# Infini-attention with two feed-forward layers: the second layer's down products follow three items behind, and finished banks are copied out in the middle of an activation

## The chip, the cores and the metric

The kernel runs on one core of one Trainium2 chip. The metric is the device time of one execution in microseconds (us), as a median over runs. The core has five engines with a queue each: TensorE (PE in the rows, its weight loads are PEld), VectorE (DVE), ScalarE (ACT), GpSimd (POOL) and SyncE (SP), which issues most DMA transfers. An engine works through its queue in order and meets the others through semaphores.

## What is computed

The reference, cut to what matters:

```python
def reference(**kwargs):
    attn_out = _attn_ref(**attn_kwargs)            # causal attention mixed with a memory term, (4, 8, 576, 64)
    x = attn_out.transpose(0, 2, 1, 3).reshape(2304, 512)
    x = _moe_ref(x=x, **moe_kwargs)                # layer 1
    return _moe2_ref(x=x, **moe2_kwargs)           # layer 2

def _moe2_ref(x, w_in, w_out):                     # x 2304 x 512, w_in 512 x 2048, w_out 2048 x 512
    h = x @ w_in
    g = h - np.tanh(h)
    return (g @ w_out).astype(np.float32)
```

The change touches layer 2 alone.

## The kernel before, in words

Attention, the conversion of the weights and layer 1 are placed by a planner (`Schedule`), which writes their order from costs and due times; that part of the program is left as it is. Layer 2 follows it in an order written out by hand, in the loop of lines 1165 to 1175.

Layer 2 takes the tokens in rounds: four rounds of 512 tokens and a last one of 256 (`rounds`, line 1013). Inside a round the 2048 hidden columns are taken 128 at a time (`f`, 16 of them; in the last round two at a time). One such step is an item: 64 items of the wide rounds and 8 of the last one, 72 in all (`items`, lines 1151 and 1152). All matrix products are made in three parts (high by high, high by low, low by high), since each operand is held as a rounded part and a remainder.

For one item:

- `up2(i)` (L1116): 12 products on TensorE (24 narrower ones in the last round) write h, 128 hidden columns by 512 tokens, into one of four PSUM banks (`up2_p`, tile `up`).
- `act2(i)` (L1077 to L1097): ScalarE and VectorE turn h into g = h - tanh(h), by a polynomial for small values. ScalarE makes `u` (L1085), `w` (L1086), `w` again (L1090), `th` (L1091) and `mk` (L1092); VectorE makes `hu` (L1087), `gf` (L1093, L1094), takes `th` from h in place (L1095, tile `up`) and merges both (L1096), which ends the item's activation.
- `act2_end(i)` (L1099): the item's g is split: ScalarE writes the rounded part `gh` (L1103), and GpSimd the remainder `gl` (L412; VectorE for the last item). It is not issued with its own item but behind `u`, `w` and `hu` of the next one, through `state["late"]`.
- `down2(i)` (L1131, products at L1142): 12 products add g's share to the output banks `dn0` to `dn3`, three for each of four token tiles of 128 (two tiles in the last round, with six each). The four banks are a ring of one (`dn2_p`): a new round can write a bank only when the old one's contents have been copied out.
- `out_copy(r, k)` (L1123): when a round's last item has been added, bank k is copied to a tile `ob` (even k on ScalarE, L399; odd k on VectorE, L401), and SP sends it to memory (L1129). There are two `ob` tiles, so the third copy waits for the first tile's transfer and the fourth for the second's.
- `prep2` (L1154): at items 4, 6, 8 and 10 of a round the next round's input is loaded and split.

TensorE's order around an item is `up2(i)`, then `down2(i - LAG2)` with `LAG2 = 2`; the activation of item i and the round-end copies come from the loop:

```python
        if i < len(items):
            up2(i)
            act2(i)
...
        elif "late" in state:
            act2_end(*state.pop("late"))
        if i >= LAG2:
            down2(i - LAG2)
```

Of the kernel before, what the change touches and what calls it, by code (L numbers as in the profile page):

```python
# [244 lines left out]
def kernel(  # L245
# [165 lines left out]
    def low(e, out, in_, high):  # L411
        (nc.vector if e == "dve" else nc.gpsimd).tensor_tensor(out=out, in0=in_, in1=high, op=ALU.subtract)  # L412
# [418 lines left out]
        return first  # L831


    LAG2 = 2
    state = {}

    def up_mms(xs, ps, p):
# [185 lines left out]
    def load2(r, i):  # L1023
        x = late["x2"].tile([128, KT, 256], F32, name="x2i")
        nc.sync.dma_start(out=x, in_=x2s[rounds[r][i]])
        state[2, r, i, "x"] = x

    def split_hi(r, i, e):
        if i == 0:
            state[2, r, "xs"] = late["xs2"].tile([128, 2, KT, 512], F32R, name="xs")  # L1030
        xs, x = state[2, r, "xs"], state[2, r, i, "x"]
        copy(e, xs[:, 0, :, 256 * i:256 * i + 256], x)

    def split_lo(r, i):
        xs, x = state[2, r, "xs"], state.pop((2, r, i, "x"))
        part = slice(256 * i, 256 * i + 256)
        nc.vector.tensor_tensor(
            out=xs[:, 1, :, part], in0=x, in1=xs.bitcast(F32)[:, 0, :, part], op=ALU.subtract)
# [38 lines left out]
    def act2(i):  # L1077
        h = state.pop((2, i, "up"))
        u = t_p.tile([128, 512], F32, name="u")
        w = t_p.tile([128, 512], F32, name="w")  # L1080
        th = t_p.tile([128, 512], F32, name="th")
        hu = t_p.tile([128, 512], F32, name="hu")
        mk = t_p.tile([128, 512], F32, name="mk")
        g = t_p.tile([128, 512], F32, name="gf")
        nc.scalar.activation(out=u, in_=h, func=AF.Square)  # L1085
        nc.scalar.activation(out=w, in_=u, func=AF.Square, bias=sqb_t)  # L1086
        nc.vector.scalar_tensor_tensor(out=hu, in0=h, scalar=c4, in1=u, op0=ALU.mult, op1=ALU.mult)  # L1087
        if "late" in state:
            act2_end(*state.pop("late"))
        nc.scalar.activation(out=w, in_=w, func=AF.Square, bias=sqc_t)  # L1090
        nc.scalar.activation(out=th, in_=h, func=AF.Tanh)  # L1091
        nc.scalar.activation(out=mk, in_=u, func=AF.Relu, bias=thr_t)  # L1092
        nc.vector.scalar_tensor_tensor(out=g, in0=u, scalar=lin, in1=w, op0=ALU.mult, op1=ALU.add)  # L1093
        nc.vector.scalar_tensor_tensor(out=g, in0=g, scalar=off, in1=hu, op0=ALU.add, op1=ALU.mult)  # L1094
        nc.vector.tensor_tensor(out=h, in0=h, in1=th, op=ALU.subtract)  # L1095
        nc.vector.copy_predicated(out=g, mask=mk.bitcast(I32), data=h)  # L1096
        state["late"] = (i, g)  # L1097

    def act2_end(i, g):  # L1099
        gl = g2_p.tile([128, 512], F32R, name="gl")  # L1100
        gh = g2_p.tile([128, 512], F32R, name="gh")
        state[2, i, "g"] = (gh, gl)
        nc.scalar.activation(out=gh, in_=g, func=AF.Copy)  # L1103
        low("dve" if i == len(items) - 1 else "pool", gl, g, gh.bitcast(F32))

    def up2(i):
        r, fs = items[i]
        xs = state[2, r, "xs"]
        n = 512 // len(fs)
        ps = up2_p.tile([128, 512], F32, name="up")  # L1110
        state[2, i, "up"] = ps
        for s, f in enumerate(fs):
            w = wt[0][f]
            for kt in range(KT):
                for j, (wh, xh) in enumerate(((0, 0), (0, 1), (1, 0))):
                    nc.tensor.matmul(  # L1116
                        ps[:, s * n:(s + 1) * n], lhsT=w[:, wh * 512 + kt * 128:wh * 512 + (kt + 1) * 128],
                        rhs=xs[:, xh, kt, 0:n], start=(kt == 0 and j == 0), stop=(kt == KT - 1 and j == 2))

    def token_tiles(r):  # L1120
        return [(n, t) for n in rounds[r] for t in range(2)]

    def out_copy(r, k):  # L1123
        n, t = token_tiles(r)[k]
        last = r == len(rounds) - 1
        ob = ob_p.tile([128, 512], F32, name="ob")
        copy("dve" if k % 2 and not last else "act", ob, state["dn"][k])
        for j, (row, r0, nr) in enumerate(out_rows(n, t)):
            (nc.scalar if last and j else nc.sync).dma_start(out=out[row:row + nr, :], in_=ob[r0:r0 + nr, :])  # L1129

    def down2(i):  # L1131
        r, fs = items[i]
        if fs[0] == 0:
            state["dn"] = [dn2_p.tile([128, 512], F32, name=f"dn{k}") for k in range(len(token_tiles(r)))]
        gh, gl = state.pop((2, i, "g"))
        n = 512 // len(fs)
        end = fs[-1] == NF - 1
        for k, dn in enumerate(state["dn"]):
            for j, (g, wh) in enumerate(((gh, 0), (gh, 1), (gl, 0))):
                for s, f in enumerate(fs):  # L1140
                    c0 = s * n + k * 128
                    nc.tensor.matmul(  # L1142
                        dn, lhsT=g[:, c0:c0 + 128], rhs=wt[1][f][:, wh * 512:(wh + 1) * 512],
                        start=(fs[0] == 0 and s == 0 and j == 0), stop=(f == NF - 1 and j == 2))
            if end and r == len(rounds) - 1:
                out_copy(r, k)
        if end and r < len(rounds) - 1:
            for k in range(len(state["dn"])):
                out_copy(r, k)

    items = [(r, (f,)) for r in range(WIDE) for f in range(NF)]
    items += [(WIDE, (2 * p, 2 * p + 1)) for p in range(NP)]

    def prep2(r, step):  # L1154

        if r + 1 < len(rounds) and step // 2 < len(rounds[r + 1]):
            i = step // 2
            if step % 2 == 0:
                load2(r + 1, i)
            else:  # L1160
                split_hi(r + 1, i, "act")
                split_lo(r + 1, i)

    PREP = {4: 0, 6: 1, 8: 2, 10: 3}
    for i in range(len(items) + LAG2):
        if i < len(items):
            up2(i)
            act2(i)
            r, fs = items[i]
            if len(fs) == 1 and fs[0] in PREP:  # L1170
                prep2(r, PREP[fs[0]])
        elif "late" in state:
            act2_end(*state.pop("late"))
        if i >= LAG2:
            down2(i - LAG2)


# [42 lines left out]
```

## Time and profile before

| | |
|---|---|
| time, median of 3 runs | 1079.64 us (1079.57 to 1081.4) |
| the profiled execution's own time | 1081.9 us |
| its span | 1080.1 us |
| TensorE busy, matrix products | 1044.4 us, 97% of the span |
| VectorE, ScalarE, GpSimd busy | 757.9, 631.8 and 99.8 us |
| layer 2, first up product to the end | from 661.43 us on, about 419 us |

How to read it: a busy share is an average over the whole program. For a change to layer 2 alone, what counts is where TensorE stands still in layer 2 and for whom; the waits, the timeline and the table by stretches show that. Times in the rows are microseconds from the start of the span.

### The profile page before, as it was taken

To read this page: it belongs to the slowest core of one execution; us is meant where nothing else is said; L and a number is where in the kernel's file an instruction comes from. 1 tells how busy PE (TensorE), PEld (TensorE's weight loads), DVE (VectorE), ACT (ScalarE), POOL (GpSimd) and SP (SyncE) were. 2 spreads that over 40 slices of the span, in tenths; PEclk is the share of its full clock that TensorE was granted. 3 is DMA by queue.
4 is the path that set the end of the run, shared out by engine and by line. 5 is a ranking of instruction groups with operands and counts; after the bars stand their busy time and mean duration, and the time that the engine had idled before them with its cause. 6 is when DMAs were issued, how large, how long until landed. Compare 5 with 4: busy or idle time off the path is not lost.

```text
span 1080.1 us, 18824 instructions
## 1 busy us (share of the span) xinstructions
PE 1044.4 (97%) x6720; PEld 881.9 (82%) x6720; DVE 757.9 (70%) x2060; ACT 631.8 (58%) x1346; POOL 99.8 (9%) x102
## 2 busy tenths in 40 slices
PE   5799999999999999999999999999999999999997
PEld 3477798777779978979999998888788788878896
DVE  6999999878776587663221377776677677767775
ACT  6889876777673376362111124666566666666674
POOL 0001000000000000000000000222122122212221
PEclk9799999999999999999999999999999999999999
DMA  7867753555644354242100164000100100010010
GB/s 229 257 176 218 236 178 114 157 149 157 189 126 150 123 161 146 88 128 73 40 1 21 40 187 145 1 21 1 58 20 1 59 20 1 1 59 1 1 40 20
DMA packets 116397, 102.42 MB, mean 95 GB/s; under 512 B 63824, under 2 KB 92496, under 8 KB 116304
## 3 DMA queue, kind: packets, MB, share of 16 engines
q1 hardware_dynamic: 115088, 99.91, 30.5%
q10 hardware_dynamic: 1216, 1.31, 0.4%
q8 instruction: 53, 0.87, 0.3%
q14 instruction: 40, 0.33, 0.1%
HBM read 78.65 MB, written 22.54 MB: 94 GB/s over the span
## 4 chain that ended last, share of the span: by engine, by line
PE 64%; issue 20%; DMA 5%; ACT 5%; DVE 4%; SPq 1%; POOL 0%; DVEq 0%; ACTq 0%; POOLq 0%
PE up L1116 17%; PE dn L1142 17%; PE dn L947 9%; PE up L845 9%; PE s L703 3%; PE s L584 3%; PE o L725 3%; PE s L589 1%; PE o L670 1%; ACT e L630 1%; DMA qk<-in_qkt_dram 1%; DMA vs<-cv 1%; ACT e L647 1%; DMA w<-in_moe_w_in_dram 1%; PE s L547 1%
## 5 line engine op out<-in xcount | busy, mean ns | idle before, releaser
L845 PE MATMUL up<-xs,w 128*128 128x256 f32 x1728 | 236.4, 287 | 0.4 <-ACT g L924 0.4
L845 PEld LDWEIGHTS up<-xs,w 128*128 128x128 f32 x1728 | 217.6, 192 | 7.0 <-issue 5.6
L1116 PE MATMUL up<-xs,w 128*128 128x512 f32 (+1 forms) x960 | 214.4, 374 | 0.0
L1116 PEld LDWEIGHTS up<-xs,w 128*128 128x128 f32 x960 | 168.5, 188 | 35.2
L1142 PE MATMUL dn<-w,gh 128*128 128x512 f32 x576 | 179.2, 397 | 7.3 <-DVE ob L401 4.7
L947 PE MATMUL dn<-gh,w 128*128 128x256 f32 x1152 | 160.1, 286 | 0.0
L947 PEld LDWEIGHTS dn<-gh,w 128*128 128x128 f32 x1152 | 146.0, 192 | 7.2 <-issue 6.5
L1093 DVE SCALAR_TENSOR_TENSOR gf<-u,w 128x512 f32<-128x512 f32 x72 | 84.1, 1169 | 79.2 <-ACT w L1090 79.2
L412 POOL TENSOR_TENSOR gl<-gf,gh 128x512 fp32r<-128x512 f32 x71 | 91.7, 1292 | 512.3 <-ACT gh L1103 512.3
L924 ACT ACTIVATE g<-up 128x512 f32<-128x512 f32 x72 | 42.9, 595 | 160.8 <-PE up L845 145.6
L1142 PEld LDWEIGHTS dn<-w,gh 128*128 128x128 f32 x576 | 107.8, 189 | 34.8 <-DVE ob L401 7.3
L1085 ACT ACTIVATE u<-up 128x512 f32<-128x512 f32 x72 | 43.0, 598 | 120.8 <-PE up L1116 120.8
L1142 PE MATMUL dn<-w,gl 128*128 128x512 f32 x288 | 110.3, 392 | 0.6 <-POOL gl L412 0.6
L630 ACT ACTIVATE e<-e,mx 128x128 f32<-128x128 f32 (+4 forms) x144 | 82.7, 577 | 10.4 <-DVE mx L610 4.4
L401 DVE CAST gh<-g 128x512 fp32r<-128x512 f32 x36 | 15.4, 427 | 101.6 <-ACT g L924 101.6
L947 PE MATMUL dn<-gl,w 128*128 128x256 f32 x576 | 84.5, 285 | 0.0
L947 PEld LDWEIGHTS dn<-gl,w 128*128 128x128 f32 x576 | 75.2, 192 | 2.1 <-issue 1.9
L610 DVE CUSTOM_DVE_ANT_0 e<-s,mask 128x128 f32<-128x128 f32 (+4 forms) x144 | 63.7, 484 | 10.4 <-PE s L584 6.5
L703 PE MATMUL s<-identr,e 128*128 128x128 f32 x448 | 64.4, 289 | 4.3 <-ACT pT L399 2.8
L399 ACT ACTIVATE pt<-s 128x320 f32<-128x320 f32 (+4 forms) x149 | 58.2, 435 | 17.4 <-PE s L691 8.7
L584 PE MATMUL s<-qk 64*128 64x128 f32 (+3 forms) x256 | 55.8, 513 | 12.2 <-DMA qk<-in_qkt_dram 10.0
L1142 PEld LDWEIGHTS dn<-w,gl 128*128 128x128 f32 x288 | 54.4, 189 | 13.6 <-POOL gl L412 1.1
(101 smaller groups left out, 1435.9 us busy)
## 6 DMA issues: line engine op xcount, KB each, us to landing
w<-in_moe_w_out_dram SPq DMA_DIRECT2D x16, 512.0 KB, 5.1
cv<-in_moe_w_in_dram SPq DMA_DIRECT2D x32, 256.0 KB, 2.8
vs<-cv SPq DMA_DIRECT2D x64, 128.0 KB, 1.8
cv<-in_moe_w_out_dram SPq DMA_DIRECT2D x32, 256.0 KB, 2.8
w<-vs SPq DMA_DIRECT2D x32, 256.0 KB, 2.7
w<-in_moe_w_in_dram SPq DMA_DIRECT2D x14, 512.0 KB, 4.9
qk<-in_qkt_dram SPq DMA_DIRECT2D x16, 448.0 KB, 3.6
v<-in_v_dram SPq DMA_DIRECT2D x16, 320.0 KB, 3.6
```

The source lines that it names most:

```text
L399: nc.scalar.activation(out=out, in_=in_, func=AF.Copy)
L412: (nc.vector if e == "dve" else nc.gpsimd).tensor_tensor(out=out, in0=in_, in1=high, op=ALU.subtract)
L584: nc.tensor.matmul(ss[j].tile[:, c0:c0 + nn], lhsT=qk.tile[p, a:a + 128], rhs=qk.tile[p, kc:kc + nn], start=True, stop=True)
L610: nc.vector.tensor_tensor_reduce(out=out, in0=in0, in1=in1, scale=-scale, scalar=mx.tile[:, 0:1] if t == 4 and j else BIG, op0=ALU.add, op ...
L630: nc.scalar.activation(out=x, in_=x, func=AF.Exp, scale=-1.0, bias=mx.tile[:, k:k + 1], accum_out=sm.tile[:, j:j + 1])
L703: nc.tensor.transpose(ss[j].tile[:, a:a + 128], x, ident)
L845: nc.tensor.matmul(ps()[:, s, :], lhsT=w[:, wh * 512 + kt * 128:wh * 512 + (kt + 1) * 128], rhs=xs()[:, xh, kt, :], start=(kt == 0 and j = ...
L947: nc.tensor.matmul(dn[m // 2].tile[:, m % 2, :], lhsT=w[:, wh * 512 + m * 128:wh * 512 + (m + 1) * 128], rhs=gg.tile[:, s * 256:(s + 1) * ...
L1085: nc.scalar.activation(out=u, in_=h, func=AF.Square)
L1093: nc.vector.scalar_tensor_tensor(out=g, in0=u, scalar=lin, in1=w, op0=ALU.mult, op1=ALU.add)
L1116: nc.tensor.matmul(ps[:, s * n:(s + 1) * n], lhsT=w[:, wh * 512 + kt * 128:wh * 512 + (kt + 1) * 128], rhs=xs[:, xh, kt, 0:n], start=(kt = ...
L1142: nc.tensor.matmul(dn, lhsT=g[:, c0:c0 + 128], rhs=wt[1][f][:, wh * 512:(wh + 1) * 512], start=(fs[0] == 0 and s == 0 and j == 0), stop=(f ...
```

## The change

`LAG2` goes from 2 to 3. `act2` becomes a generator that stops once, behind `u`, `w`, `hu` and the late split of the item before; the loop runs it to that point, then issues `down2` of the item three behind (with the copies at a round's end), and then the rest of the activation. `prep2` moves behind `down2`. No instruction is added or taken away.

```diff
-    LAG2 = 2
+    LAG2 = 3
...
         if "late" in state:
             act2_end(*state.pop("late"))
+        yield
         nc.scalar.activation(out=w, in_=w, func=AF.Square, bias=sqc_t)
...
             up2(i)
-            act2(i)
-            r, fs = items[i]
-            if len(fs) == 1 and fs[0] in PREP:
-                prep2(r, PREP[fs[0]])
+            steps = act2(i)
+            next(steps)
         elif "late" in state:
             act2_end(*state.pop("late"))
         if i >= LAG2:
             down2(i - LAG2)
+        if i < len(items):
+            for _ in steps:
+                pass
+            r, fs = items[i]
+            if len(fs) == 1 and fs[0] in PREP:
+                prep2(r, PREP[fs[0]])
```

The line numbers behind line 1087 grow by one, and those of the loop by a few.

TensorE, at the start of layer 2 (`up` with `w_n` is the up product of item n, `dn` with `w_n` the down product of item n). Before:

```order
L1116 MATMUL up<-xs,w_0_276 128x512 x12
L1116 MATMUL up<-xs,w_1_329 128x512 x12
L1116 MATMUL up<-xs,w_2_534 128x512 x12
L1142 MATMUL dn_8899<-w_0_428,gh 128x512 x2
L1142 MATMUL dn_8899<-w_0_428,gl 128x512
```

Now:

```order
L1117 MATMUL up<-xs,w_0_276 128x512 x12
L1117 MATMUL up<-xs,w_1_329 128x512 x12
L1117 MATMUL up<-xs,w_2_534 128x512 x12
L1117 MATMUL up<-xs,w_3_592 128x512 x12
L1143 MATMUL dn_8925<-w_0_428,gh 128x512 x2
L1143 MATMUL dn_8925<-w_0_428,gl 128x512
```

Four items' up products now stand ahead of the first down product, where three stood. From there on each down product stands one item later.

ScalarE, at the end of the first round (`ob<-dn0` and `ob<-dn2` are the copies of banks 0 and 2). Before:

```order
L1085 ACTIVATE u_9567<-up_9554 128x512
L1086 ACTIVATE w_9568<-u_9567,sqb_t_73 128x512
L1103 ACTIVATE gh_9577<-gf_9527 128x512
L1090 ACTIVATE w_9568<-w_9568,sqc_t_74 128x512
L1091 ACTIVATE th_9569<-up_9554 128x512
L1092 ACTIVATE mk_9571<-u_9567,thr_t_75 128x512
L399 ACTIVATE ob_9599<-dn0_8899 128x512
L399 ACTIVATE ob_9605<-dn2_8901 128x512
L1085 ACTIVATE u_9624<-up_9611 128x512
```

Now:

```order
L1085 ACTIVATE u_9600<-up_9587 128x512
L1086 ACTIVATE w_9601<-u_9600,sqb_t_73 128x512
L1104 ACTIVATE gh_9610<-gf_9560 128x512
L399 ACTIVATE ob_9625<-dn0_8925 128x512
L399 ACTIVATE ob_9631<-dn2_8927 128x512
L1091 ACTIVATE w_9601<-w_9601,sqc_t_74 128x512
L1092 ACTIVATE th_9602<-up_9587 128x512
L1093 ACTIVATE mk_9604<-u_9600,thr_t_75 128x512
L1085 ACTIVATE u_9657<-up_9644 128x512
```

Three instructions of the item's activation, which stood ahead of the two copies, now stand behind them.

VectorE, at the same place (banks 1 and 3). Before:

```order
L1087 SCALAR_TENSOR_TENSOR hu_9570<-up_9554,u_9567 128x512
L1093 SCALAR_TENSOR_TENSOR gf_9572<-u_9567,w_9568 128x512
L1094 SCALAR_TENSOR_TENSOR gf_9572<-gf_9572,hu_9570 128x512
L1095 TENSOR_TENSOR up_9554<-up_9554,th_9569 128x512
L1096 COPY_PREDICATED gf_9572<-mk_9571,up_9554 128x512
L401 COPY ob_9602<-dn1_8900 128x512
L401 COPY ob_9608<-dn3_8902 128x512
```

Now:

```order
L1087 SCALAR_TENSOR_TENSOR hu_9603<-up_9587,u_9600 128x512
L401 COPY ob_9628<-dn1_8926 128x512
L401 COPY ob_9634<-dn3_8928 128x512
L1094 SCALAR_TENSOR_TENSOR gf_9605<-u_9600,w_9601 128x512
L1095 SCALAR_TENSOR_TENSOR gf_9605<-gf_9605,hu_9603 128x512
L1096 TENSOR_TENSOR up_9587<-up_9587,th_9602 128x512
L1097 COPY_PREDICATED gf_9605<-mk_9604,up_9587 128x512
```

Both copies pass four instructions of the activation. The same move is made at the ends of the other three wide rounds; the order of SP and GpSimd stays.

## Rows read from the trace of the kernel before

**Rows 1.** The page's part 4: the chain that ended last, by engine.

```profile
PE 64%; issue 20%; DMA 5%; ACT 5%; DVE 4%; SPq 1%; POOL 0%; DVEq 0%; ACTq 0%; POOLq 0%
```

**Rows 2.** Waits, layer 2 (660 to 1080 us): total us, times, longest.

```profile
ACT ob L399 <- DMA out_dram<-ob: 8.6, 4, 2.2
...
PE dn L1142 <- DVE ob L401: 4.7, 6, 1.2
...
PE dn L1142 <- ACT gh L1103: 2.6, 2, 1.4
```

**Rows 3.** Busy time by stretches, inside the second round.

```profile
core 0: us, PE busy (x) PEld busy (x) DVE busy (x) ACT busy (x) POOL busy (x), PEclk, DMA share, GB/s
...
775.00:846.00 71.00, 71.00 (x307) 57.47 (x306) 51.97 (x66) 47.01 (x79) 16.10 (x13) 1.00 0.02 8
```

**Rows 4.** Timeline of TensorE, start of layer 2: start, us, what, [idle before <-releaser].

```profile
661.43 8.56 PE L1116 MATMUL up<-xs,w 128*128 128x512 f32 x36
671.36 0.74 PE L1142 MATMUL dn<-w,gh 128*128 128x512 f32 x2 [1.37 <-ACT gh L1103]
672.72 0.74 PE L1142 MATMUL dn<-w,gl 128*128 128x512 f32 x1 [0.62 <-POOL gl L412]
...
676.70 2.96 PE L1116 MATMUL up<-xs,w 128*128 128x512 f32 x12
679.50 0.63 PE L1142 MATMUL dn<-w,gh 128*128 128x512 f32 x2
...
682.26 2.98 PE L1116 MATMUL up<-xs,w 128*128 128x512 f32 x12
```

**Rows 5.** Busy time by stretches, behind the first stall: the clock column.

```profile
673.26:674.50 1.24, 1.24 (x4) 0.99 (x3) 1.24 (x2) 0.96 (x2) 0.00 (x0) 0.50 0.00 0
```

**Rows 6.** Timeline of ScalarE and GpSimd, start of layer 2.

```profile
661.44 1.09 ACT L399 ACTIVATE g<-dn 128x512 f32<-128x512 f32 x2 [3.88 <-issue]
...
670.67 0.63 ACT L1103 ACTIVATE gh<-gf 128x512 fp32r<-128x512 f32 x1 [0.58 <-DVE gf L1096]
...
671.38 1.28 POOL L412 TENSOR_TENSOR gl<-gf,gh 128x512 fp32r<-128x512 f32 x1 [206.47 <-ACT gh L1103]
```

**Rows 7.** Timeline of TensorE, end of the first round.

```profile
760.28 2.98 PE L1116 MATMUL up<-xs,w 128*128 128x512 f32 x12
...
763.10 0.63 PE L1142 MATMUL dn<-w,gh 128*128 128x512 f32 x2
...
764.32 0.74 PE L1142 MATMUL dn<-w,gh 128*128 128x512 f32 x2 [0.37 <-DVE ob L401]
...
767.19 0.74 PE L1142 MATMUL dn<-w,gh 128*128 128x512 f32 x2 [1.20 <-DVE ob L401]
...
768.01 2.96 PE L1116 MATMUL up<-xs,w 128*128 128x512 f32 x12
```

**Rows 8.** Timeline of ScalarE and VectorE, end of the first round.

```profile
758.36 0.69 DVE L1087 SCALAR_TENSOR_TENSOR hu<-up,u 128x512 f32<-128x512 f32 x1 [0.22 <-ACT u L1085]
...
758.99 0.62 ACT L1103 ACTIVATE gh<-gf 128x512 fp32r<-128x512 f32 x1
...
759.51 0.71 ACT L1090 ACTIVATE w<-w,sqc_t 128x512 f32<-128x512 f32 x1
...
761.21 0.58 ACT L399 ACTIVATE ob<-dn 128x512 f32<-128x512 f32 x1
...
762.96 0.74 DVE L1096 COPY_PREDICATED gf<-mk,up 128x512 f32<-128x512 int32 x1
...
763.59 0.68 DVE L401 COPY ob<-dn 128x512 f32<-128x512 f32 x1
763.94 0.60 ACT L399 ACTIVATE ob<-dn 128x512 f32<-128x512 f32 x1 [2.15 <-DMA out_dram<-ob]
...
766.44 0.69 DVE L401 COPY ob<-dn 128x512 f32<-128x512 f32 x1 [2.17 <-DMA out_dram<-ob]
```

**Rows 9.** Timeline of TensorE, the last two items' down products.

```profile
1068.22 1.08 PE L1142 MATMUL dn<-w,gh 128*128 128x512 f32 x4
...
1072.38 1.19 PE L1142 MATMUL dn<-w,gh 128*128 128x512 f32 x4 [1.24 <-ACT gh L1103]
```

## The prediction

> **What bounds the kernel now.** I read the chain of waits first: TensorE holds 64% of the chain that ended last [rows 1], so time is won only where TensorE stands still or runs slowly. The table by stretches comes next. In the 71 us from 775 on TensorE is busy all 71.00, at full clock, while VectorE works 51.97 and ScalarE 47.01 [rows 3]. Inside a round nothing but the matrix products counts. An item takes 2.80 for its up products (676.70 to 679.50) and 2.76 for the down products (679.50 to 682.26) [rows 4], 5.56 together. In that time VectorE has about 5.56 x 19.03 / 71 = 1.5 us to spare and ScalarE 5.56 x 23.99 / 71 = 1.9.
>
> The waits of layer 2 then say where TensorE does stand: 4.7 us for a copy `ob`, and 2.6 for `gh` in two pieces [rows 2]. The timeline places them: the layer's start, the ends of rounds and the layer's end. I price each by starts against the undisturbed pace, because a stop also costs something behind itself.
>
> **The change part by part.**
>
> The start. Three items' up products begin at 661.43 and need 3 x 2.80; the first down products then wait 1.37 for `gh` and 0.62 for `gl`, and the next up products begin at 676.70 [rows 4]. At pace they would have begun at 661.43 + 8.40 + 2.76 = 672.59, so the start loses 4.11. Only 1.99 of it is idle. In the stretch behind the stall the granted clock is 0.50, the 1.2 GHz level [rows 5], so much of the rest is products at half speed. Now a fourth item's up products come first, and the down products begin at 661.43 + 4 x 2.80 = 672.63. `gh` has been written by 671.30, and `gl` by 672.66 [rows 6]; a bank's first two products use `gh`, the third `gl`, two thirds of 0.69 later. Margins are 1.3 and 0.4 us. ScalarE's and VectorE's orders are the same up to there. I take the whole 4.11. The fourth item's bank is one that layer 1 left, whose last copies end at 662.53 [rows 6], before TensorE gets there at 669.83.
>
> Ends of rounds. Down products of a new round begin at 763.10, wait 0.37 before bank 1 and 1.20 before bank 3, and the next up products begin at 768.01 [rows 7]. That is 4.91 in place of 2.76, a loss of 2.15. The 4.7 of the waits is three times 0.37 + 1.20, so three ends are alike; behind the fourth wide round there are only two banks to wait for, and the end costs nothing. The cause is in the copies: bank 0's copy begins only behind the activation, at 761.21, bank 1's at 763.59, bank 2's waits 2.15 for the first transfer, bank 3's 2.17 for the second [rows 8].
>
> With the change, in the same times: the round's last down products end at 760.28, where the next up products begin [rows 7], and the banks are done at 0.69 steps, bank 0 at 758.2, bank 1 at 758.9. ScalarE is free for bank 0 where it now takes up the second `w`, at 759.51; the copy ends at 760.09. VectorE ends `hu` at 759.05 [rows 8] and copies bank 1 until about 759.8. Bank 2's copy starts 2.15 behind the first one's end, at 762.25, and ends at 762.85. Bank 3's starts 2.17 behind the second one's; SP issues that transfer behind the other, so I count from 760.1: it starts at 762.3 and ends at 763.0, with a few tenths more for the issue. TensorE wants bank 2 at 760.28 + 2.80 + 1.38 = 764.46 and bank 3 at 765.15. Margins are 1.6 and about 2 us. I take all three losses: 3 x 2.15 = 6.45.
>
> What is queued behind the copies. The rest of item i's activation, which ran from 759.51 to 763.70 (4.19 us) [rows 8], now starts at 762.85 at the earliest, 3.34 later, and ends near 767.05. Then `gh` takes 0.63 and `gl` 1.28 [rows 6], until 769.0. These products are wanted three items behind, at 760.28 + 3 x 2.80 + 2 x 2.76 = 774.2: a margin of 5.2 us. The item's up bank is wanted again after that. With 1.5 us to spare in each item, VectorE has made good the 3.34 within three items; the next round end is 16 items away. Cost nothing; if the cover were gone, 3.34 at each of four ends.
>
> The end. Item 70's down products begin at 1068.22, item 71's at 1072.38, after 1.24 of idle for `gh` [rows 9]. At pace it would be 2.76, so 1.40 is lost. Three items' down products, in place of two, now stand between the last up products and item 71's: 2.76 more cover against 1.40. I take 1.40.
>
> `prep2` moves behind `down2` in the program, but it falls on items 4 to 10 of a round and the copies on item 2, so no queue changes by it; SP's and GpSimd's orders stay. Three `gh` and three `gl` tiles still do: the tile that item i writes was read by item i - 3, whose products end before item i + 1's up products begin. Cost nothing.
>
> **Sum:** 4.11 + 6.45 + 1.40 = 11.96 us. The profiled execution, 1081.9 with 1.8 around its span, would come to 1069.9. It lies 2.3 above the median of the runs; taken from the median of 1079.64 it is 1067.7, which is my forecast. I take no more than the sum: the rest of layer 2 is at pace already.
>
> **A rule that speaks against it.** In these rows ScalarE's second copy stands 2.15 for a transfer while the next item's work is behind it [rows 8]; that is the hold which the change puts into the middle of an activation. The Trainium skill, "PSUM — Partial Sum Buffer", section "Engine vs sequencer instructions", says that the queues of ScalarE, VectorE and GpSimd are strict FIFO, so that nothing behind a blocked copy can pass it. By that rule, the trace agrees; alone it would hand the hold on to TensorE (the second rival's time), by the margin in the rows it does not.
>
> **The rivals.**
>
> *The copies stay too late.* If the transfers take over 1.6 us longer than 2.15, bank 2 is late again. For it: the two waits for transfers stay, 8.6 us over four ends on ScalarE [rows 2]. Against: all four of those are at most 2.2. At worst the 6.45 stays lost: 1074.1.
>
> *The hold reaches TensorE (slower).* ScalarE and VectorE stand at the copies with the activation behind them, `gh` comes late, and the copy wait is exchanged for a wait for `gh` at all four wide ends. Without cover that is 4 x 3.34 = 13.4 against the 11.96 won: 1081.1; if each stop drags the clock down as at the start, where 1.99 of idle cost 4.11, it is 27.6 and 1095. It decides where `gl` comes so late that each end loses 3.0 us, that is 5.2 + 3.0 = 8.2 later than reckoned (6.6 if the clock doubles the loss). Against it: the longest wait that these rows show inside an activation is 2.2 us.
>
> *The start is not covered.* The fourth item's up products wait (for a bank or for their weights), or `gl` slips beyond its 0.4 us. The 4.11 stays at worst: 1071.8. For it is the thin margin alone.
>
> *Nothing comes of it.* Stalls move to places that the rows do not show, and the median stays near 1079.6. Against: each of the five stops has its releaser and its new cover.
>
> **How the numbers follow.** Forecast 0.82; copies late 0.06; start not covered 0.06; hold reaches TensorE 0.04; nothing 0.02. The range goes up to 1074.1, which takes in the two partial cases, and down to 1065.5: the three runs lie within 1.8 us of each other, and that much below the forecast is room for the measurement. About 0.2% (2.2 us) is what a measurement of this kernel can tell from no change. Faster by more than that: 0.82 + 0.06 + 0.06 = 0.94; within it 0.02; slower 0.04.
>
> **What would show it.** In the profile of the changed kernel: four items' up products in a row (48) at the layer's start with the first down products right behind them and no clock below 1.00; no wait of TensorE for `ob` at the round ends, with the copies of banks 0 and 1 running while the round's last products still do, and the third and fourth still waiting near 2.15 for transfers; `gf` at L1094 late by about 3.3 us once a round; the last item's down products without idle. The forecast is wrong if TensorE waits for `gh` or `gl` two to four items behind a round end, if a bank's copy still ends after TensorE wants it, or if layer 2 takes more than 410 us.

## The result and the profile after

| | before | changed |
|---|---|---|
| time, median of the runs | 1080.12 us (4 runs, 1079.57 to 1081.4) | 1070.28 us (4 runs, 1068.74 to 1071.82) |
| ratio | | 0.9907, 95% interval 0.9889 to 0.9926 |
| profiled execution | 1081.9 us, span 1080.1 | 1068.74 us, span 1067.0 |
| layer 2, first up product to the end of the span | 418.67 us | 406.56 us |

The kernel is 9.8 us faster in the medians (8.0 to 12.0 by the interval). The forecast was 1067.7 with a range of 1065.5 to 1074.1. A second set of four runs of the changed kernel, below, has a median of 1069.43 beside 1080.18. Layer 2 of the profiled executions became shorter by 418.67 - 406.56 = 12.11 us; the sum was 11.96. (Spans are read to a tenth of a us, so stretches that go to the end of the span are good to about 0.1.)

Both kernels' layer 2, as one stretch each, in the table by stretches (columns as in [rows 3]); first before, then after:

```profile
661.43:1080.10 418.67, 406.01 (x1826) 329.92 (x1824) 295.59 (x380) 270.29 (x453) 91.71 (x71) 0.99 0.07 23
```

```profile
660.44:1067.00 406.56, 401.84 (x1826) 329.46 (x1824) 293.56 (x380) 271.47 (x453) 92.00 (x71) 1.00 0.07 24
```

TensorE was without work for 12.66 us of the layer before, and for 4.72 now; the 4.72 are the last copies and transfers, behind its last product. Its busy time fell by 4.2 with the same 1826 recorded products, since before some ran at the 1.2 GHz level [rows 5] and the first ones behind a stop took longer (0.74 for a pair that takes 0.63 elsewhere, [rows 7]).

The waits of the changed kernel in layer 2 (total us, times, longest) answer to [rows 2]:

```profile
DVE ob L401 <- DMA out_dram<-ob: 12.5, 4, 3.1
...
ACT ob L399 <- DMA out_dram<-ob: 8.6, 4, 2.2
```

There is no line in which TensorE's products wait. The copies still wait for transfers, VectorE even longer than before (12.5 us in all, against 8.7), and no product waits for them.

The start of layer 2, timeline of TensorE:

```profile
660.44 11.35 PE L1117 MATMUL up<-xs,w 128*128 128x512 f32 x48
671.63 0.62 PE L1143 MATMUL dn<-w,gh 128*128 128x512 f32 x2
...
674.38 2.98 PE L1117 MATMUL up<-xs,w 128*128 128x512 f32 x12
```

Four items' up products run in a row, and the down products begin 11.19 behind the first, at pace; in [rows 4] they began at 9.93 for three items, 1.5 late, and then stopped once more.

The end of the first round, all engines but the weight loads; it answers to [rows 7, 8]:

```profile
756.05 0.69 DVE L1087 SCALAR_TENSOR_TENSOR hu<-up,u 128x512 f32<-128x512 f32 x1 [0.23 <-ACT u L1085]
...
756.81 0.69 DVE L401 COPY ob<-dn 128x512 f32<-128x512 f32 x1
...
757.20 0.58 ACT L399 ACTIVATE ob<-dn 128x512 f32<-128x512 f32 x1
...
757.98 2.98 PE L1117 MATMUL up<-xs,w 128*128 128x512 f32 x12
759.95 0.60 ACT L399 ACTIVATE ob<-dn 128x512 f32<-128x512 f32 x1 [2.17 <-DMA out_dram<-ob]
760.45 0.71 ACT L1091 ACTIVATE w<-w,sqc_t 128x512 f32<-128x512 f32 x1
760.63 0.69 DVE L401 COPY ob<-dn 128x512 f32<-128x512 f32 x1 [3.12 <-DMA out_dram<-ob]
760.80 0.63 PE L1143 MATMUL dn<-w,gh 128*128 128x512 f32 x2
...
763.39 0.75 DVE L1097 COPY_PREDICATED gf<-mk,up 128x512 f32<-128x512 int32 x1
763.55 2.98 PE L1117 MATMUL up<-xs,w 128*128 128x512 f32 x12
...
764.24 0.63 ACT L1104 ACTIVATE gh<-gf 128x512 fp32r<-128x512 f32 x1 [0.73 <-DVE gf L1097]
...
764.95 1.29 POOL L412 TENSOR_TENSOR gl<-gf,gh 128x512 fp32r<-128x512 f32 x1 [6.28 <-ACT gh L1104]
...
771.94 0.63 PE L1143 MATMUL dn<-w,gh 128*128 128x512 f32 x2
```

Banks 0 and 1 are copied while the round's last products still run (the next up products begin at 757.98), banks 2 and 3 are free at 760.55 and 761.32. The new round's products begin at 760.80 and take 763.55 - 760.80 = 2.75, the undisturbed time, where they took 4.91. The item whose activation is held has its `gl` at 764.95 + 1.29 = 766.24, and its down products begin at 771.94, 5.7 later.

The end of the layer, TensorE, answers to [rows 9]:

```profile
1058.04 1.07 PE L1143 MATMUL dn<-w,gh 128*128 128x512 f32 x4
1058.94 0.62 PE L1143 MATMUL dn<-w,gl 128*128 128x512 f32 x2
1059.39 1.07 PE L1143 MATMUL dn<-w,gh 128*128 128x512 f32 x4
1060.30 0.62 PE L1143 MATMUL dn<-w,gl 128*128 128x512 f32 x2
1060.76 1.07 PE L1143 MATMUL dn<-w,gh 128*128 128x512 f32 x4
```

These are the second half of item 70's down products and all but the last two of item 71's. They follow each other without idle; in [rows 9] item 71's waited 1.24.

### The profile page after: what moved, and what is told of

Its sections match the earlier page's. It is cut to its first block, busy times and chain, and to the rows that moved or that the text cites. A ratio compares the mean times of both kernels' runs of the same rounds, so it can differ in the third digit from the quotient of the medians.

```text
span 1067.0 us, 18825 instructions
## 1 busy us (share of the span) xinstructions
PE 1036.7 (97%) x6720; PEld 879.5 (82%) x6720; DVE 755.8 (71%) x2060; ACT 633.0 (59%) x1346; POOL 100.0 (9%) x102
## 4 chain that ended last, share of the span: by engine, by line
PE 86%; DMA 5%; DVE 3%; ACT 3%; issue 1%; SPq 1%; ACTq 0%; DVEq 0%
PE up L1117 19%; PE dn L1143 19%; PE dn L947 18%; PE up L845 18%; PE o L725 3%; PE s L703 3%; PE s L584 3%; DMA vs<-cv 2%; PE s L589 1%; PE o L670 1%; DMA cv<-in_moe_w_out_dram 1%; ACT e L630 1%; DMA w<-in_moe_w_in_dram 1%; DVE e L610 1%; PE s L547 1%
## 5 line engine op out<-in xcount | busy, mean ns | idle before, releaser
L1094 DVE SCALAR_TENSOR_TENSOR gf<-u,w 128x512 f32<-128x512 f32 x72 | 84.0, 1167 | 70.6 <-ACT w L1091 70.6
```

## The experiments

My theory is the sum of the prediction: three separate losses, each with a cover of its own, and a hold of the activation that costs nothing. The numbers to compare are layer 2's stretches, from the first up product to the end of the span; the times of whole runs of one kernel differ by up to 5 us.

### The lag alone

```diff
-    LAG2 = 2
+    LAG2 = 3
```

(on the kernel before)

> Down products three items behind, activation and copies in the order of the kernel before. If the sum is right (start 4.11, ends of rounds 3 x 2.15, end 1.40), the start and the end are won and the ends of rounds stay: layer 2, from its first up product to the end of the span, takes 418.67 - 5.5 = 413.2 us, about 1074.6 in all; TensorE waits for ob at three round ends (0.37 + 1.20 each) and for gh or gl nowhere. Rival (the lag alone gives all, the copies' place matters nothing): about 406.6 us. Rival (the start is not covered): 417.3.

Measured: layer 2 412.88 us (660.92 to 1073.8); 1076.38 us in the median of 6 runs beside 1080.41, ratio 0.9962 (0.9946 to 0.9977). The waits for `gh` and `gl` are gone, those of the round ends are as before. Timeline of TensorE at the first one:

```profile
761.28 0.63 PE L1142 MATMUL dn<-w,gh 128*128 128x512 f32 x2
...
762.51 0.74 PE L1142 MATMUL dn<-w,gh 128*128 128x512 f32 x2 [0.37 <-DVE ob L401]
...
765.37 0.73 PE L1142 MATMUL dn<-w,gh 128*128 128x512 f32 x2 [1.18 <-DVE ob L401]
...
766.16 2.96 PE L1116 MATMUL up<-xs,w 128*128 128x512 f32 x12
```

766.16 - 761.28 - 2.76 = 2.12 is lost, about what [rows 7] gave (2.15). The lag by itself does nothing for the copies.

### The copies' place alone

```diff
-    LAG2 = 3
+    LAG2 = 2
```

(on the changed kernel)

> Copies in the middle of the activation, down products two items behind as before. If the sum is right, the three waits for ob go and the start and the end stay as before: 418.67 - 6.45 = 412.2 us for layer 2, with the idle for gh and gl of 2.6 and 0.6 us as before. With one item less of cover, gl of the held item should come about 0.5 us ahead of its product. Rival (the hold needs the third item): a new wait for gl or gh of 0.5 to 3 us behind each of the four round ends, 414 us or more.

Measured: layer 2 412.02 us (662.08 to 1074.1); 1075.48 us in the median of 5 runs, ratio 0.9945 (0.9928 to 0.9961). No product waits for `ob` any more, and no wait for `gl` or `gh` appears behind the round ends. Its held item at the first one, GpSimd, then TensorE:

```profile
767.56 1.29 POOL L412 TENSOR_TENSOR gl<-gf,gh 128x512 fp32r<-128x512 f32 x1 [6.27 <-ACT gh L1104]
...
769.00 0.63 PE L1143 MATMUL dn<-w,gh 128*128 128x512 f32 x2
...
769.47 0.39 PE L1143 MATMUL dn<-w,gl 128*128 128x512 f32 x1
```

`gl` is there at 768.85, 0.6 us ahead of its product. So the copies' new place does not need the third item, but only just. The two parts add up within 0.4: 418.67 - 412.88 = 5.79 and 418.67 - 412.02 = 6.65, 12.44 together, against 12.11 for both.

### Four tiles for the copies: is the hold free?

```diff
-    ob_p = late_pool("ob", 2)
+    ob_p = late_pool("ob", 4)
...
-        th = t_p.tile([128, 512], F32, name="th")
+        th = t_p.tile([128, 512], F32, name="th", bufs=1)
...
-        mk = t_p.tile([128, 512], F32, name="mk")
+        mk = t_p.tile([128, 512], F32, name="mk", bufs=1)
```

(on the changed kernel)

> The changed kernel with four ob tiles (and one th and one mk tile, to make room), so that no copy waits for a transfer and ScalarE and VectorE aren't held. If the hold is wholly covered, as the sum has it, nothing changes: 406.6 us for layer 2 within 0.3, though the waits of ob for transfers (8.6 and 12.5 us) are gone. Rival (the hold costs TensorE something): up to 2 us less.

Measured: layer 2 406.56 us, no difference that the profile can show; 1069.46 us in the median of 4 runs, ratio 0.9896 (0.9882 to 0.9911). The copies' waits are now these:

```profile
ACT ob L399 <- PE dn L1143: 3.6, 2, 2.8
DVE ob L401 <- PE dn L1143: 2.7, 4, 0.7
```

21.1 us of waiting for transfers were taken away from ScalarE and VectorE, and TensorE gained nothing. The single `th` and `mk` tiles hide no gain here: with them and two copy tiles (four items behind, below) the layer took 406.49. The hold of some 3 us is wholly covered.

### One tile for the copies: a longer hold

```diff
-    ob_p = late_pool("ob", 2)
+    ob_p = late_pool("ob", 1)
```

(on the changed kernel)

> The changed kernel with one ob tile: the four copies run one behind the other with a transfer of about 2.2 us between, and the activation is held for about 8 us. If only the banks' lateness counts, TensorE waits for bank 2 about 1.3 and for bank 3 about 2.2 at three round ends, with some 0.2 more of restart: 3.7 each, 406.56 + 11 = 417.7 us for layer 2, and no wait for gh or gl. Rival (the hold reaches TensorE through gh and gl): such waits at all four ends, over 420. Rival (each stop of this length also halves the clock behind it): about 7 each, 428.

Measured: layer 2 425.76 us; 1090.05 us in the median of 4 runs, ratio 1.0087 (1.0072 to 1.0102). That is 8 us over my number. TensorE at the first round end, and the products behind the second:

```profile
764.93 0.73 PE L1143 MATMUL dn<-w,gh 128*128 128x512 f32 x2 [1.08 <-ACT ob L399]
...
767.79 0.73 PE L1143 MATMUL dn<-w,gh 128*128 128x512 f32 x2 [1.90 <-DVE ob L401]
...
768.59 2.96 PE L1117 MATMUL up<-xs,w 128*128 128x512 f32 x12
...
861.35 4.50 PE L1117 MATMUL up<-xs,w 128*128 128x512 f32 x12
```

The first end went as expected: down products begin at 762.29, so 768.59 - 762.29 - 2.76 = 3.54 is lost, all for banks. At the second and third the granted clock fell as well. In the table by stretches, behind the second end:

```profile
861.35:865.68 4.33, 4.33 (x13) 3.38 (x12) 3.36 (x5) 2.33 (x4) 1.29 (x1) 0.61 0.51 181
```

The up products begin at 861.35 and their down products at 865.68, 4.33 in place of 2.81; with the bank waits this end costs 5.12, the third 6.23. The rest, 4.37, is lost at the layer's end: the fourth hold comes with too few items left to make it good (behind it `u` starts every 4.83 us where TensorE takes 5.65 for an item, so 0.82 is won back per item), `gh` is late for the last item, and the last copy waits for the one before it. TensorE, then ScalarE, at that end:

```profile
1074.53 0.73 PE L1143 MATMUL dn<-w,gl 128*128 128x512 f32 x2 [0.17 <-POOL gl L412]
...
1077.98 1.21 PE L1143 MATMUL dn<-w,gh 128*128 128x512 f32 x4 [1.34 <-ACT gh L1104]
```

```profile
1083.04 0.60 ACT L399 ACTIVATE ob<-dn 128x512 f32<-128x512 f32 x1 [2.75 <-DMA out_dram<-ob]
```

3.54 + 5.12 + 6.23 + 4.37 = 19.26 accounts for the 425.76 - 406.56 = 19.20. So a long hold does cost, by banks first (at all three ends), by `gh` only near the end of the program; behind the three other ends no product waited for `gh` or `gl`, although at the first of them the held item's `gh` started 6.9 us late (770.61, where 758.18 + 5.57 would be in step).

### The kernel before with four tiles

```diff
-    ob_p = late_pool("ob", 2)
+    ob_p = late_pool("ob", 4)
```

(on the kernel before, with one `th` and one `mk` tile as above)

> The kernel before (two items behind, copies behind the whole activation) with four ob tiles (and one th and one mk tile, to make room). If the waits at the round ends come from the ring of two ob tiles, only bank 1's late first copy stays: 0.37 of idle and 0.24 of restart at three ends, a loss of 0.6 each in place of 2.15, layer 2 at 418.67 - 3 x 1.55 = 414.0 us. If they come from where the copies stand alone, the loss stays 2.15 each, 418.7 us.

Measured: layer 2 411.90 us; 1075.28 us in the median of 5 runs, ratio 0.9954 (0.9937 to 0.9972). TensorE at the first round end:

```profile
757.77 2.98 PE L1116 MATMUL up<-xs,w 128*128 128x512 f32 x12
...
761.81 0.72 PE L1142 MATMUL dn<-w,gh 128*128 128x512 f32 x2 [0.37 <-DVE ob L401]
...
763.99 2.96 PE L1116 MATMUL up<-xs,w 128*128 128x512 f32 x12
```

763.99 - 757.77 - 2.81 - 2.76 = 0.65 is lost, as expected: the larger part of a round end's 2.15 comes from the ring of two tiles, the smaller from the late first copy. The layer is 2.1 shorter than I expected, though, and that lies at its start, whose order this edit leaves as it was:

```profile
661.20 8.56 PE L1116 MATMUL up<-xs,w 128*128 128x512 f32 x36
670.41 0.73 PE L1142 MATMUL dn<-w,gh 128*128 128x512 f32 x2 [0.66 <-ACT gh L1103]
671.77 0.50 PE L1142 MATMUL dn<-w,gl 128*128 128x512 f32 x1 [0.63 <-POOL gl L412]
...
674.17 2.98 PE L1116 MATMUL up<-xs,w 128*128 128x512 f32 x12
```

674.17 - 661.20 - 8.40 - 2.76 = 1.81, where the same sum over [rows 4] gave 4.11.

### Four items behind

```diff
-    LAG2 = 3
+    LAG2 = 4
...
-    g2_p = late_pool("g2", 3)
+    g2_p = late_pool("g2", 4)
```

(on the changed kernel, with one `th` and one `mk` tile)

> The changed kernel with down products four items behind (four gh and gl tiles; one th and one mk tile, to make room). If nothing of the cover is short at three, nothing is won: 406.6 us for layer 2 within 0.3. Rival (three is still too short somewhere): up to 1 us less. Rival (four items' h waiting in four banks hold up the up products): some us more, with waits of up products for the activation.

Measured: layer 2 406.49 us; 1069.14 us in the median of 4 runs, ratio 0.9898 (0.9882 to 0.9915). Nothing is short at three.

### The changed kernel again

> The changed kernel once more, beside these: layer 2 at 406.6 us within 0.3, the ratio of the times between 0.988 and 0.992. If layer 1's stretch differs from run to run, the span moves with it while layer 2's stays.

Measured: layer 2 406.56 us; 1069.43 us in the median of 4 runs (1069.33 to 1069.71) beside 1080.18, ratio 0.9903 (0.9888 to 0.9917). Layer 2 is the same within the 0.1 of the reading in three profiles (this one, the first and the one with four tiles), though it began at 661.24, 660.44 and 660.74.

### Three more profiles of the kernel before

> The kernel before once more, for its layer 2 alone. If the start's loss of 4.11 us is a constant, layer 2 takes 418.7 us again. If it depends on how far behind the activation is when layer 1 ends, and on whether the clock falls, as the losses of 3.60 and 1.81 in two experiments that leave the start alone suggest, it lies between 416.3 and 418.7, and the rest (round ends 6.45, end 1.40) is the same.

> As the first look: 418.7 us if the start is a constant, 416.3 to 418.7 if it isn't.

> As the first look: 418.7 us if the start is a constant, 416.3 to 418.7 if it isn't.

Measured: layer 2 416.93, 416.67 and 419.15 us. By the same sum as above the start loses 2.29, 2.12 and 4.59. TensorE in the second and the third of these profiles:

```profile
660.33 8.56 PE L1116 MATMUL up<-xs,w 128*128 128x512 f32 x36
669.85 0.73 PE L1142 MATMUL dn<-w,gh 128*128 128x512 f32 x2 [0.96 <-ACT gh L1103]
671.21 0.50 PE L1142 MATMUL dn<-w,gl 128*128 128x512 f32 x1 [0.62 <-POOL gl L412]
...
673.61 2.98 PE L1116 MATMUL up<-xs,w 128*128 128x512 f32 x12
```

```profile
661.45 8.56 PE L1116 MATMUL up<-xs,w 128*128 128x512 f32 x36
671.88 0.73 PE L1142 MATMUL dn<-w,gh 128*128 128x512 f32 x2 [1.87 <-ACT gh L1103]
673.24 0.80 PE L1142 MATMUL dn<-w,gl 128*128 128x512 f32 x1 [0.62 <-POOL gl L412]
...
677.20 2.96 PE L1116 MATMUL up<-xs,w 128*128 128x512 f32 x12
```

The loss is not a constant. In the third the idle is longer, and the products behind it run slowly (granted clock 0.72 over 671 to 677); in the second they run at 1.00.

What makes the idle differ stands in ScalarE's queue, ahead of `gh`: two waits for transfers that the planner's part of the program issues. ScalarE in the profile of [rows 4]:

```profile
664.66 0.63 ACT L399 ACTIVATE w<-w 128x512 fp32r<-128x512 f32 x1 [1.61 <-DMA w<-vs]
...
666.27 0.72 ACT L1086 ACTIVATE w<-u,sqb_t 128x512 f32<-128x512 f32 x1 [0.49 <-DMA x2s<-g]
```

The two add up to 2.10 there, to 1.83, 1.71 and 2.61 in the three profiles of this section, and to 1.37 (the kernel before with four tiles) and 1.78 (the copies' place alone). TensorE's idle for `gh` was 1.37, 1.11, 0.96, 1.87, 0.66 and 1.04: 0.71 to 0.75 less each time. In the second profile of the changed kernel they add up to 2.12, as late as in [rows 4], and no product waits: the fourth item's up products cover it. A start as late as the third profile's was not met with three items behind; there `gl`'s first product began at 673.24, and the changed order would want it at 661.45 + 4 x 2.80 + 0.46 = 673.11 (0.46 for the bank's two products with `gh`), so by this estimate the cover would be just used up.

## Why the prediction was right, and where it was off

**The direction and the mechanism** were right, term by term. In the profiled pair layer 2 gave 12.11 against a sum of 11.96.

**The round ends**, 3 x 2.15 = 6.45: the copies' place alone gave 6.65, of which 0.51 is a start that lost 3.60 instead of 4.11, so 6.14 is left. Bank 2 was free at 760.55 where I would have it at 762.85 - 760.28 + 757.98 = 760.55. Bank 3 came 0.6 later than I had it, 761.32 against 760.7: VectorE waited 3.12 from its first copy's end, not 2.17 from ScalarE's. TensorE wanted it at 760.80 + 2.07 = 762.87, so the margin was 1.5, not 2, and still enough.

**The start and the end**, 4.11 + 1.40 = 5.51: the lag alone gave 5.79.

**The hold** was priced at nothing with a margin of 5.2 us. The profile shows 5.7, with `gf` at L1094 3.2 late (761.26, where one item later than 752.44 + 5.57 would be 758.01; 3.3 was expected). Removing the waits for transfers changed nothing (406.56 both times), and even with one item less of cover no product behind a round end waited. The rival in which the hold reaches TensorE falls at its place, the wide ends; with the longer hold of one copy tile it shows only at the program's end. Making the delay good took longer than the three items reckoned from VectorE's 1.5 us to spare: `u` is in step again two items behind the first round end (1.2 late one item behind), but `gf`'s last step on VectorE (L1097) is 2.74 late with the held item, then 1.99, 1.25, 0.51 and 0. That is 0.74 per item, since an activation follows the next after 4.83 (as with one copy tile) where TensorE's item takes 5.57: VectorE still waits 0.87 or more for ScalarE's `w` in each of them. It cost nothing, with sixteen items to a round. Nothing passed a blocked copy in either trace: in the changed kernel ScalarE's second `w` needs only the first, which was done at 756.78, and it starts at 760.45, behind the copy that had stood 2.17. What such a hold costs is decided by the cover behind it.

**The other rivals.** The copies were not late, the start was covered (in all profiles with the lag of three or four, no product waits there), and the stalls did not come up elsewhere.

**What was off** is the step "taken from the median of 1079.64 it is 1067.7": a sum with the start's 4.11 of one profiled execution was carried over to the median. That execution was one of the long starts. Over the six profiles with two items behind (the first, the one with four tiles, the three of the section above, the one with the copies' place alone) it lost 4.11, 1.81, 2.29, 2.12, 4.59 and 3.60. With the 2.1 of the short kind (1.81 to 2.29) in place of 4.11, the sum is 6.45 + 1.40 + 2.1 = 9.95, and the time 1079.64 - 9.95 = 1069.7, between the two medians measured, 1070.28 and 1069.43. Which kind the timed runs of before had is not seen, since they have no trace; that part is argued. The four profiled executions of before point that way: 1081.9 and 1082.34 us with a long start, 1079.53 and 1078.78 with a short one, and the medians of before, 1079.64 to 1080.41, lie nearer the latter. (Part of these differences lies ahead of layer 2, which began at 661.43, 661.45, 660.87 and 660.33.) The prediction's other figure, the profiled execution less its sum, 1069.9, was nearer to what was measured.

## What to carry to other kernels

Where one engine is the bound and everything else has slack, list each of its stops with what releases it, price a stop by the starts of the work around it and not by its idle alone, and ask for each whether the edit puts other work of that engine in front of it: the three sorts of stop here had two separate cures, which added up. A blocked copy in the middle of other work costs nothing as long as what stands behind it is wanted later than the wait; count that margin in the bound engine's own items, as 0.6 us was left with two items of cover and 5.7 with three. Before a sum from one profiled execution is taken off a median, see whether the stretch that it rests on repeats: here one term was 2.1 in one profile of the same kernel and 4.6 in another, by when two transfers had landed and whether the clock fell.

## What the runs showed of the hardware that was not expected

The granted clock behind a stop of TensorE is not settled by how long the engine stood. At the start of layer 2 it stayed at 1.00 behind waits of 1.11 and 0.63 us (the first of the three further profiles of before), of 0.96 and 0.62 and of 0.66 and 0.63, and fell to 0.50 behind 1.04 and 0.61 (the copies' place alone), behind 1.37 and 0.62 [rows 4, 5] and behind 1.87 and 0.62 (the third). With one copy tile, three round ends with nearly the same waits (1.08 and 1.90, 1.14 and 1.90, 1.15 and 1.88) read 1.00, 0.61 and 0.60 in the 4 us or so behind. No fall was seen behind the 0.37 and 1.20 of the round ends before. What decides it stays open. The clock column alone is not the speed either: in the profile with four items behind it reads 0.95 in stretches all over the program (0.95 over layer 2), and the same 1826 products were busy 401.78 us there, against 401.84 at a reading of 1.00.
